# A gated sum of an FFT filter and a state-space model: the scan over odd tokens only, complex products summed on VectorE before the inverse transform, and copies of the turned x on VectorE

## The chip, the cores and the metric

The kernel runs on one core of a Trainium2 chip. The metric is device microseconds of one execution of the whole program, the median of several timed runs. Beside the timed runs there is one profiled execution; its trace gives the start and the duration of every instruction. Engines are named as the profile names them: PE is TensorE (matmuls; PEld its weight loads), DVE is VectorE, ACT is ScalarE, POOL is GpSimd, SP is SyncE, whose queue issues most of the DMAs.

## The reference

One input x of 2048 tokens by 1024 features, in bf16, goes through two branches, and a gate per token mixes them.

```python
g = sigmoid((x * gate_w).sum(-1, keepdims=True))

# branch A: a filter in the frequency domain
X = rfft2(x)                                   # 2048 x 513, complex
a = irfft2(X * (w_r + 1j * w_i), s=(2048, 1024))

# branch B: a diagonal complex state-space model, 1024 states
Lam_bar = exp(dt * Lam)
Bu = einsum("ld,pd->lp", x, ((Lam_bar - 1) / Lam)[:, None] * Bmat)
for t in range(2048):
    h = Lam_bar * h + Bu[t]
    hs.append(h)
b = 2 * einsum("lp,dp->ld", hs, Cmat).real + x * Dskip

return g * a + (1 - g) * b
```

## The kernel before

**Branch B** goes by chunks of `TC` = 256 tokens, eight of them (`c` from 0 to 7). `unit_mm` multiplies x by B on PE into PSUM, real and imaginary parts apart, and `unit_out` has ACT copy it into a tile `h` of [128, 2 (re, im), 8, 256] in bf16: 1024 states are 8 blocks of 128 partitions, and time lies along the free axis. The complex recurrence is made real by turning: a table `tab` holds, per state and per time inside the chunk, the cosine and sine of the angle that the state has turned through, so that after a rotation the recurrence has the real decay r alone. All of this is DVE's and lies in `recur`: `cross` and `along` (two products of 4096 elements per partition), `join_re` and `join_im` rotate in; `carry_in` adds the state from the chunk before into the first time step; `scan` runs h = r h + u along time, once for the real and once for the imaginary part, 2048 elements each (the decay table `rz` is zero at the first time of a block, so that one instruction goes over eight blocks); `carry_part` and `carry_sum` make the carry for the next chunk; and `cross`, `along`, `out_re`, `out_im` rotate back. Chunks 0 and 1 are done in two halves of four blocks each (`NSEP`), so these instructions are half as long there. `c_half` and `c_part` then multiply `h` by C on PE; time is the stationary side, 128 tokens (`tq`) at once.

**Branch A** is a two-dimensional FFT by matmuls. `turn` transposes x by PE into PSUM (`pt`, bf16) in 12 blocks of 128 tokens, and `turn_out` has ACT copy each into `xQ` (the last four blocks come transposed by a DMA, and ACT copies these as well). `fold` makes sums and differences on DVE, `fd` multiplies by the transform over features, `fd_out` evacuates, `s1` is the first step over tokens and `s1_out` evacuates it. By `FD_DVE` and `S1_DVE`, seven of these 32 evacuations are on DVE, the others on ACT. A turn through DRAM follows, then for eight groups `g`: `s2` on PE, `s2_out` on ACT into `X2`, `times_w` on DVE, `is1` on PE. `times_w` multiplies X (re, im) by W's real part and by its imaginary part, 2048 products per tile, two tiles `b` per group; the four kinds of product stay apart, and `is1` sums them as four accumulating steps with four variants of the matrix `MT`: 32 matmuls per group. `is2` and `is2_out` bring the result into `ZT`, and `spectral_mm`, `spectral_out`, `spectral` are the inverse transform over features, token block by token block (`tb`, 16 of 128 tokens).

**Closing.** For token blocks 0 to 9 the two branches meet through DRAM: `early_out` stores (1 - g) y, `scale_skip` and `add_skip` add the skip term to it, and `add_late` adds it to the spectral part by DMAs from POOL's queue. The last blocks meet in SBUF; blocks 13 to 15 are the end of the program: `skip_last` and `last_out` on DVE read the last C products from PSUM, and `last_store` stores them.

**Order.** Nothing is scheduled by the program that builds the kernel. Every step is a generator, and the string `ORDER` says letter by letter which one makes its next piece; `PIECES` says in which order the pieces of `recur` come (the letter `v`), and `SLOTS` which of four PSUM homes each PSUM tile takes. Each engine works through its own instructions in the order in which they were made, and each SP, ACT or POOL DMA stands in its engine's queue.

## Time and profile before

| what | value |
|---|---|
| median of 3 timed runs | 305.25 us (305.02 to 307.25) |
| profiled execution: first to last instruction | 303.6 us |
| PE busy | 296.4 us, 2568 matmuls |
| DVE busy | 289.3 us, 340 instructions |
| ACT busy | 188.5 us, 255 instructions |
| POOL busy | 73.3 us |
| granted TensorE clock | 1.00 but for the last 14 us (0.97) |
| DMA | 59.35 MB, mean 196 GB/s |

The profile gives no other time of its own than the span of its instructions; the median of the timed runs is 1.65 us above it. Busy time of PE counts overlapping matmuls once, and the ends of matmuls are modelled; DVE's busy time is the union of its instructions. A row of a group reads: line, engine, operation, written and read tiles, partitions x elements, count | total busy us, mean ns of one | idle time before.

### The profile page before, as it was taken

How to read it: one execution, taken by the hardware profiler on the slowest of the kernel's cores; microseconds unless marked ns; L12 is line 12 of the kernel's file. 1: busy time of each engine (PE TensorE's matmuls, PEld its weight loads, DVE VectorE, ACT ScalarE, POOL GpSimd, SP SyncE). 2: the span in 40 equal slices, each digit the busy share in tenths (PEclk: the TensorE clock that was granted, in tenths of full speed). 3: DMA queues.
4: the chain of work that ended last, by engine and by line, in shares of the span. 5: the costliest groups of instructions: out<-in, count | busy, mean ns of one | idle time of the engine just before them, and what ended most of it. 6: DMA issues, size and time to landing. Idle time of an engine off the chain costs nothing. (4 is left out here: it accounts for less than half of the span.)

```text
span 303.6 us, 6402 instructions
## 1 busy us (share of the span) xinstructions
PE 296.4 (98%) x2568; PEld 197.4 (65%) x2592; DVE 289.3 (95%) x340; ACT 188.5 (62%) x255; POOL 73.3 (24%) x99
## 2 busy tenths in 40 slices
PE   8999999999999999999999999999999999999995
PEld 5664677878864685458553866669657986645543
DVE  2999999999999999999999999999899999999995
ACT  4999999896532383667665865529668774343400
POOL 2100420745893001110210220202011253252330
PEclk9999999999999999999999999999999999999999
DMA  6999999989999599895948798687758876978976
GB/s 208 341 201 194 253 193 310 162 142 154 268 214 241 160 259 219 181 250 189 212 96 258 163 223 225 139 294 147 242 174 185 165 88 135 160 132 143 165 153 181
DMA packets 74157, 59.35 MB, mean 196 GB/s; under 512 B 44904, under 2 KB 61680, under 8 KB 74128
## 3 DMA queue, kind: packets, MB, share of 16 engines
q1 hardware_dynamic: 66560, 49.82, 65.8%
q0 software_dynamic: 6912, 8.69, 23.0%
q10 hardware_dynamic: 656, 0.44, 0.5%
q8 instruction: 20, 0.33, 0.4%
q14 instruction: 9, 0.07, 0.1%
HBM read 27.46 MB, written 23.08 MB: 166 GB/s over the span
## 5 line engine op out<-in xcount | busy, mean ns | idle before, releaser
L398 PE MATMUL psu<-xQ,BT 128*128 128x256 bf16 x1024 | 116.5, 273 | 0.2 <-DVE X L449 0.2
L398 PEld LDWEIGHTS <-BT 128*128 128x128 bf16 x1024 | 99.0, 98 | 17.3 <-issue 4.6
L713 PE MATMUL ps_y<-CT,h 128*128 128x512 bf16 x397 | 92.5, 379 | 0.9
L363 DVE TENSOR_TENSOR_SCAN h<-rz,h 128x2048 bf16<-128x2048 f32 (+1 forms) x20 | 70.8, 3561 | 0.0
L713 PEld LDWEIGHTS <-h 128*128 128x128 bf16 x416 | 39.6, 98 | 46.3 <-issue 2.9
L785 POOL DMA_DIRECT2D y_scratch<-su x20 | 17.3, 902 | 135.7 <-ACT su L779 105.4
L408 ACT CAST h<-psu 128x1024 bf16<-128x1024 f32 x32 | 32.3, 1011 | 18.7 <-PE psu L398 13.1
L350 DVE TENSOR_TENSOR h<-h,tab 128x4096 bf16<-128x4096 bf16 (+1 forms) x20 | 37.1, 1859 | 0.1
L744 ACT ACTIVATE ye<-ps_y,omg 128x512 f32<-128x512 f32 x26 | 17.9, 689 | 26.3 <-PE ps_y L713 11.8
L347 DVE TENSOR_TENSOR xQ<-h,tab 128x4096 bf16<-128x4096 bf16 x12 | 27.4, 2284 | 1.0 <-ACT h L408 1.0
L603 ACT CAST X<-ps_s 128x1024 bf16<-128x1024 f32 x16 | 16.2, 1010 | 14.6 <-PE ps_s L594 11.2
L727 PE MATMUL ps_q<-CT,h 128*128 128x512 bf16 (+2 forms) x110 | 21.3, 348 | 0.2
L817 ACT ACTIVATE BT<-ps_id,gB 128x1024 bf16<-128x1024 f32 x14 | 15.3, 1114 | 9.9 <-PE ps_id L810 5.7
L671 ACT CAST ZT<-ps_is 128x1024 bf16<-128x1024 f32 x16 | 15.8, 1017 | 6.2 <-PE ps_is L661 6.2
L637 ACT CAST C<-ps_is 128x1024 bf16<-128x1024 f32 x16 | 15.7, 1011 | 5.1 <-DMA xQ<-in_A_x_dram 3.4
L851 POOL DMA_DIRECT2D BT<-y_scratch x10 | 13.1, 1452 | 19.7 <-DVE BT L846 13.3
L727 PEld LDWEIGHTS <-h 128*128 128x128 bf16 x112 | 10.3, 98 | 10.4 <-DVE h L378 0.5
L779 ACT ACTIVATE su<-xs,omg 128x512 f32<-128x512 bf16 x20 | 14.2, 723 | 4.1 <-DMA y_scratch<-su 2.2
L929 ACT COPY xQ<-pt 128x1024 bf16<-128x1024 bf16 x12 | 12.2, 1082 | 1.3 <-PE pt L919 1.3
L449 ACT CAST X<-ps_fd 128x1024 bf16<-128x1024 f32 x12 | 12.3, 1062 | 1.0 <-PE ps_fd L439 0.9
L617 DVE TENSOR_TENSOR UV<-X,Wb 128x2048 bf16<-128x2048 bf16 x8 | 9.6, 1220 | 0.6 <-ACT ye L744 0.6
L617 DVE TENSOR_TENSOR UV<-X,raw 128x2048 bf16<-128x2048 bf16 x8 | 9.8, 1223 | 0.2 <-ACT X L604 0.2
(200 smaller groups left out, 397.3 us busy)
## 6 DMA issues: line engine op xcount, KB each, us to landing
y_scratch<-ye SPq DMA_DIRECT2D x20, 256.0 KB, 4.6
y_scratch<-su POOLq DMA_DIRECT2D x20, 256.0 KB, 4.7
Bb<-turn_scratch SPq DMA_DIRECT2D x16, 256.0 KB, 5.2
turn_scratch<-C SPq DMA_DIRECT2D x16, 256.0 KB, 4.1
raw<-turn_scratch SPq DMA_DIRECT2D x8, 512.0 KB, 4.3
xs<-in_A_x_dram SPq DMA_DIRECT2D x13, 256.0 KB, 3.9
out_dram<-BT SPq DMA_DIRECT2D x11, 256.0 KB, 4.3
CT<-in_A_x_dram SPq DMA_DIRECT2D x5, 512.0 KB, 6.1
```

The costliest lines, as they stand in the source:

```text
L347: nc.vector.tensor_mul(out=tmps["s"], in0=u[:, ::-1], in1=bc(i))
L350: nc.vector.tensor_mul(out=u, in0=u, in1=bc(i))
L363: nc.vector.tensor_tensor_scan(out=seg, data0=rz[:, js.start + j:js.start + j + m].rearrange("p j t -> p (j t)"), data1=seg, initial=0.0, ...
L398: nc.tensor.matmul(psu[:, j, :], lhsT=BT[4 * q + j][:, ri, d8, :], rhs=xQ[:, c, d8, :], start=(d8 == 0), stop=(d8 == 7))
L408: nc.scalar.copy(out=hs[c][:, ri, 4 * q:4 * q + 4].rearrange("p b (q j) -> p b q j", j=32), in_=psus.pop((c, q, ri)).rearrange("p b (j q) ...
L603: nc.scalar.copy(out=X2, in_=ps2s[g][b])
L617: nc.vector.tensor_mul(out=UV, in0=X2s.pop((g, b)).unsqueeze(1).to_broadcast([P, 2, 2, K]), in1=fft["Wb"][g // 2 % 2][:, :, at:at + 1, :]. ...
L671: nc.scalar.copy(out=ZT[:, 4 * kp:4 * kp + 4, :, 4 * G:4 * G + 4].rearrange("p (c r) n g -> p c r n g", c=2), in_=pszs.pop((G, kp)).rearra ...
L713: nc.tensor.matmul(psy, lhsT=hs[c][:, ri, jb, P * tq:P * (tq + 1)], rhs=CT[ri][:, jb, 512 * dh:512 * (dh + 1)], start=(i == 0), stop=(i == ...
L727: nc.tensor.matmul(psq, lhsT=hs[c][:, ri, jb, P * tq:P * (tq + 1)], rhs=CT[ri][:, jb, at:at + n], start=(i == 0), stop=(i == 15))
L744: nc.scalar.activation(out=ye, in_=psys[tb][:, K * hf:K * (hf + 1)], func=ACT.Copy, scale=omg[:, tb:tb + 1])
L785: nc.gpsimd.dma_start(out=y_dram[tb, hf], in_=xgs[tb, hf], accum_op=ALU.add)
```

## The change

Tokens are now split into even and odd ones throughout. `h` becomes [128, 2 (even, odd), 2 (re, im), 8, 128], `tab` and `rz` likewise, and a block of 128 tokens (`tb`) is the even or the odd half of a chunk: `rows_of` picks every second row of x and of the output, still whole rows of 2 KB. In `recur`, the rotation in is as before. The odd part's table holds the extra factor for one step of decay, so that `fold_in` adds the even part to the odd part; `scan` then runs over the odd tokens alone, with the decay r squared, real and imaginary part in one instruction of 2048 elements (chunks 0 and 1: two instructions of 512 per half). `next_` has ACT write r squared times the scanned value of the odd token before into a spare tile, block by block (eight ACT instructions per chunk, four per half), and `fill_in` adds that to the even part on DVE. `carry_in` puts the carry into the spare tile's first column and `carry_add` adds the same column to the odd part; `carry_sum` is gone. The rotation back is as before.

`make_tab` makes these tables: ACT scales the odd half by r, POOL casts the even half and scales the odd half by the inverse of r squared (`rinv2`), and DVE's four instructions per pair of blocks are as many and as long as before.

`times_w` takes both tiles of a group in one product of 4096 elements per partition, and then DVE makes the complex product's real part (a subtraction) and imaginary part (an addition), 1024 elements each. `is1` sums two steps instead of four: 16 matmuls per group in place of 32, with three variants of `MT`. The tiles `X2` and `UV` are twice as large and have one buffer each instead of two. `is2` and `is2_out` write `ZT` in another layout.

x is loaded by halves of 16 tokens (`x_v`), so that `pt` comes out of the transposes in the order in which `turn_out` reads it; all 16 copies of the turned x move from ACT to DVE (`TURN_DVE`), and all the evacuations of `fd` and `s1` that were on DVE move to ACT. `ORDER`, `PIECES` and `SLOTS` are written anew for all engines.

```diff
-FD_DVE = (2, 4, 6, 7)
-CAST_ACT = (5, 6, 7)
+FD_DVE = ()
-S1_DVE = (1, 4, 5)
+S1_DVE = ()
+TURN_DVE = tuple(range(16))
...
 PIECES = (
-    0, 1, 2, 3, 4, 5, 6, 8, 7, 9, 11, 10, 24, 25, 27, 26, 12, 13, 15, 14, 17, 16, 28, 18,
+    0, 1, 3, 2, 5, 6, 4, 8, 9, 10, 7, 11, 12, 14, 13, 15, 16, 17, 18, 20, 21, 19, 24, 23, 25, 22, 26, 27, 28, 29, 30,
...
-        MT=b16(np.concatenate([-np.cos(angM), -np.sin(angM), np.cos(angM), np.sin(angM)], axis=2)),
+        MT=b16(np.concatenate([-np.sin(angM), np.cos(angM), np.sin(angM)], axis=2)),
...
-    out2 = out[0]
+    rows_of = lambda t: [t.rearrange("(c p e) d -> c e p d", p=P, e=2)[tb // 2, tb % 2] for tb in range(16)]
+    out_rows, x_rows = rows_of(out[0]), rows_of(x)
...
-    x_v = x.rearrange("(p j) d -> p j d", j=16)
+    x_v = x.rearrange("(s g j) d -> g s j d", g=2, j=16)
...
     def make_tab(jp):
...
-        cast(2 * jp)(out=tab[:, 1, js, :], in_=sn_f)
-        yield
-        t1 = tmp.tile(sh, FP32, name="t1")
-        t2 = tmp.tile(sh, FP32, name="t2")
-        for j in range(2):
-            nc.scalar.activation(out=t1[:, j], in_=sn_f[:, j], func=ACT.Copy, scale=ci[:, 2 * jp + j:2 * jp + j + 1])
-        yield
-        cast(2 * jp + 1)(out=tab[:, 0, js, :], in_=cs_f)
-        yield
+        nc.gpsimd.tensor_copy(out=tab[:, 0:2, 0, js, :], in_=sc[:, :, :, 0:TS])
+        yield
+        t = tmp.tile([P, 2, 2, TC], FP32, name="t")
         for j in range(2):
             jb = 2 * jp + j
-            nc.scalar.activation(out=t2[:, j], in_=cs_f[:, j], func=ACT.Copy, scale=ci[:, jb:jb + 1])
-        yield
+            odd = sc[:, :, j, TS:TC]
+            nc.scalar.activation(out=odd, in_=odd, func=ACT.Copy, scale=r_sb[:, jb:jb + 1])
+            nc.scalar.activation(out=t[:, j], in_=sc[:, :, j], func=ACT.Copy, scale=ci[:, jb:jb + 1])
+            yield
         for j in range(2):
             jb = 2 * jp + j
-            nc.vector.scalar_tensor_tensor(out=tab[:, 2, jb, :], in0=cs_f[:, j], scalar=cr[:, jb:jb + 1], in1=t1[:, j],
-                                           op0=ALU.mult, op1=ALU.subtract)
-            yield
...
+            nc.gpsimd.tensor_scalar_mul(out=tab[:, 0:2, 1, jb, :], in0=sc[:, :, j, TS:TC], scalar1=rinv2[:, jb:jb + 1])
+            yield
+        one = lambda z: z.rearrange("p (e s) -> p e s", e=2)
+        for i, op in ((0, ALU.subtract), (1, ALU.add)):
+            for j in range(2):
+                jb = 2 * jp + j
+                nc.vector.scalar_tensor_tensor(out=tab[:, 2 + i, :, jb, :], in0=one(sc[:, i, j]), scalar=cr[:, jb:jb + 1],
+                                               in1=one(t[:, j, 1 - i]), op0=ALU.mult, op1=op)
+                yield
...
     def recur(c, js, home):
...
-        def carry_in():
-            on_in.tensor_add(out=u[:, :, :, 0], in0=u[:, :, :, 0], in1=carry[:, :, js])
-
-        def scan(ri, j, m):
-            seg = u[:, ri, j:j + m].rearrange("p j t -> p (j t)")
-            nc.vector.tensor_tensor_scan(out=seg, data0=rz[:, js.start + j:js.start + j + m].rearrange("p j t -> p (j t)"),
-                                         data1=seg, initial=0.0, op0=ALU.mult, op1=ALU.add)
+        def carry_in():
+            first = tmps["s"][:, 0, :, :, 0]
+            if c:
+                nc.vector.tensor_add(out=first, in0=ck[:, :, 0, js], in1=ck[:, :, 1, js])
+            else:
+                nc.vector.memset(first, 0.0)
+
+        def carry_add():
+            nc.vector.tensor_add(out=u[:, 1, :, :, 0], in0=u[:, 1, :, :, 0], in1=tmps["s"][:, 0, :, :, 0])
+
+        def fold_in():
+            nc.vector.tensor_add(out=u[:, 1], in0=u[:, 1], in1=u[:, 0])
+
+        def scan():
+            flat = lambda t, i: t[:, i, js].rearrange("p j t -> p (j t)") if n < 8 else t.rearrange("p r j t -> p (r j t)")
+            for i in range(2 if n < 8 else 1):
+                seg = flat(hs[c][:, 1], i)
+                nc.vector.tensor_tensor_scan(out=seg, data0=flat(rz, i), data1=seg, initial=0.0, op0=ALU.mult, op1=ALU.add)
+
+        def next_(j):
+            for i in range(j, j + 2):
+                nc.scalar.activation(out=tmps["s"][:, 0, :, i, 1:TS], in_=u[:, 1, :, i, 0:TS - 1], func=ACT.Copy,
+                                     scale=r2_sb[:, js.start + i:js.start + i + 1])
+
+        def fill_in():
+            nc.vector.tensor_add(out=u[:, 0], in0=u[:, 0], in1=tmps["s"][:, 0])
...
-        work.extend((lambda: scan(0, 0, n), lambda: scan(1, 0, n)))
+            work.append(carry_add)
+        work.extend((fold_in, scan))
         if c + 1 < NCH:
-            work.extend((carry_part, carry_sum))
+            work.append(carry_part)
+        work.extend(partial(next_, j) for j in range(0, n, 2))
+        work.append(fill_in)
         work.extend((lambda: cross(3), lambda: along(2), out_re, out_im))
...
     def times_w():
         for g in range(8):
-            for b in range(2):
-                UV = UVs[g, b] = fft["gt"].tile([P, 2, 2, K], BF16, name="UV", tag="guv", bufs=2)
-                at = 2 * (g % 2) + b
-                nc.vector.tensor_mul(out=UV, in0=X2s.pop((g, b)).unsqueeze(1).to_broadcast([P, 2, 2, K]),
-                                     in1=fft["Wb"][g // 2 % 2][:, :, at:at + 1, :].to_broadcast([P, 2, 2, K]))
-                yield
+            UV = UVs[g] = fft["gt"].tile([P, 2, 2, 2, K], BF16, name="UV", tag="guv", bufs=1)
+            W = fft["Wb"][g // 2 % 2][:, :, 2 * (g % 2):2 * (g % 2) + 2]
+            nc.vector.tensor_mul(out=UV, in0=X2s.pop(g).unsqueeze(1).to_broadcast([P, 2, 2, 2, K]),
+                                 in1=W.unsqueeze(2).to_broadcast([P, 2, 2, 2, K]))
+            yield
+            nc.vector.tensor_sub(out=UV[:, 0, 0], in0=UV[:, 0, 0], in1=UV[:, 1, 1])
+            yield
+            nc.vector.tensor_add(out=UV[:, 0, 1], in0=UV[:, 0, 1], in1=UV[:, 1, 0])
+            yield
 
     def is1():
...
-            for i, (u, r, n) in enumerate(((0, 0, 64), (0, 1, 32), (1, 0, 32), (1, 1, 0))):
+            for r in range(2):
...
     def turn_out():
         for j in range(16):
-            if j >= NTURN:
-                nc.scalar.copy(out=x_gjq[:, :, :, :, j, :].rearrange("p c d g q -> p d g c q"),
-                               in_=xt[:, j - NTURN].rearrange("p d g (c q) -> p d g c q", c=NCH))
-                yield
-                continue
-            nc.scalar.copy(out=x_gjq[:, :, :, :, j, :].rearrange("p c d g q -> p d c g q"),
-                           in_=pts.pop(j).rearrange("p d (c q g) -> p d c g q", c=NCH, g=2))
+            if j < NTURN:
+                src = pts.pop(j).rearrange("p d (g c q) -> p d g c q", g=2, c=NCH)
+            else:
+                src = xt[:, j - NTURN].rearrange("p d g (c q) -> p d g c q", c=NCH)
+            (nc.vector.tensor_copy if j in TURN_DVE else nc.scalar.copy)(
+                out=x_gjq[:, :, :, :, j, :].rearrange("p c d g q -> p d g c q"), in_=src)
             yield
```

How the instructions move is shown at three places. In these rows `x` after a row counts equal rows that follow each other, and a scan is named SCALAR_TENSOR_TENSOR with `rz` as its first operand.

DVE before, last chunk, from the first scan (L363) to the second; L825 to L846 are the spectral part of other token blocks (`BT` is reused as their home):

```order
L363 SCALAR_TENSOR_TENSOR h<-rz,h 128x2048
L844 TENSOR_TENSOR BT<-BT 128x2x512
L846 TENSOR_TENSOR BT<-BT 128x2x512
L825 TENSOR_TENSOR BT<-BT 128x2x2x128
L827 TENSOR_TENSOR BT<-BT 128x2x2x128
L836 TENSOR_TENSOR BT<-BT 128x4x256
L838 TENSOR_TENSOR BT<-BT 128x4x256
L363 SCALAR_TENSOR_TENSOR h<-rz,h 128x2048
```

DVE with the change, last chunk, from the only scan (L366) to `fill_in` (L374); L842 to L863 are the same spectral steps:

```order
L366 SCALAR_TENSOR_TENSOR h<-rz,h 128x2048
L853 TENSOR_TENSOR BT<-BT 128x4x256
L855 TENSOR_TENSOR BT<-BT 128x4x256
L861 TENSOR_TENSOR BT<-BT 128x2x512
L863 TENSOR_TENSOR BT<-BT 128x2x512
L842 TENSOR_TENSOR BT<-BT 128x2x2x128
L844 TENSOR_TENSOR BT<-BT 128x2x2x128
L853 TENSOR_TENSOR BT<-BT 128x4x256
L855 TENSOR_TENSOR BT<-BT 128x4x256
L374 TENSOR_TENSOR h<-h,xQ 128x2048
```

The second scan is gone; between the scan and the addition that needs ACT's copies of it stand eight spectral instructions.

ACT with the change, at the same place: the eight copies of `next_` (L370) for the last chunk, among the evacuations of C products (L761) and of the spectral matmuls (L834):

```order
L834 ACTIVATE BT<-ps_id,gB 128x1024 x3
L761 ACTIVATE ye<-ps_y,omg 128x512
L370 ACTIVATE xQ<-h,r_sb 128x2x127 x6
L761 ACTIVATE ye<-ps_y,omg 128x512
L370 ACTIVATE xQ<-h,r_sb 128x2x127 x2
L761 ACTIVATE ye<-ps_y,omg 128x512
```

These eight rows are new on ACT, and one evacuation stands between the sixth and the seventh of them.

DVE with the change, first half of chunk 1, from `fold_in` (L360) to the rotation back (L338); `Bcol` belongs to a small side computation of branch A, and L378 is `carry_part`:

```order
L360 TENSOR_TENSOR h<-h 128x2x512
L366 SCALAR_TENSOR_TENSOR h<-rz,h 128x512 x2
L560 COPY Bcol<-aps 32x128
L561 TENSOR_SCALAR Bcol<-Bcol 32x64
L378 TENSOR_TENSOR ck<-h,rot 128x4x4
L374 TENSOR_TENSOR h<-h,su 128x2x512
L338 TENSOR_TENSOR su<-h,tab 128x2048
```

Before, the same half chunk had two scans of 1024 elements and no `fold_in` or `fill_in`; here three small instructions stand between the scan and `fill_in`, which needs four copies from ACT.

More of the change, by code (lines that the diff above doesn't have):

```diff
@@ L1 @@
-import itertools
+from functools import partial
 from contextlib import ExitStack
@@ L27 @@
 NCH = S // TC
+TS = TC // 2
 NEARLY = 10
@@ L1091, in turn_vectors @@
         nc.scalar.activation(out=r_sb, in_=are, func=ACT.Exp)
+        nc.scalar.activation(out=r2_sb, in_=are, func=ACT.Exp, scale=2.0)
+        nc.scalar.activation(out=rinv2, in_=are, func=ACT.Exp, scale=-2.0)
         yield
```

150 lines of the change are left out of this document (73 added, 77 removed), and 11 rows, old and new, of the table PIECES.

## The prediction

> **What bounds the kernel now.** I read the busy times first, then the stretches, the waits and the chain that ended last. The page's first part (busy us, share of the span, instructions):
>
> ```profile
> PE 296.4 (98%) x2568; PEld 197.4 (65%) x2592; DVE 289.3 (95%) x340; ACT 188.5 (62%) x255; POOL 73.3 (24%) x99
> ```
>
> Two engines are close to full. The stretches show where (columns: length, then PE, PEld, DVE, ACT and POOL busy with their instructions, granted clock, DMA share, GB/s):
>
> ```profile
> 40.00:290.00 250.00, 248.83 (x2171) 167.40 (x2189) 245.85 (x247) 153.35 (x208) 62.82 (x67) 1.00 0.89 191
> 0.00:40.00 40.00, 37.20 (x337) 24.47 (x341) 33.21 (x80) 35.15 (x48) 8.39 (x31) 1.00 1.03 236
> ```
>
> Between 40 and 290 us PE is idle for 1.2 us and DVE for 4.2. Neither has room for the other's work to grow. In the first 40 us ACT is the fuller of the two copying engines. DVE's waits (us, times, longest) say the same: the one at the start apart, all are a microsecond or less.
>
> ```profile
> DVE vecF L1082 <- PE vps L1080: 4.9, 1, 4.9
> DVE xQ L347 <- ACT h L408: 1.0, 1, 1.0
> ...
> DVE UV L617 <- ACT ye L744: 0.6, 1, 0.6
> ```
>
> The chain that ended last, in order of time (start, us, what), is DVE's own work up to the end of the last chunk's rotation, then PE's last products with C:
>
> ```profile
> 283.53 1.22 DVE h L374
> 284.75 0.33 DVE BT L825
> 285.08 0.34 DVE BT L827
> 285.42 1.15 DVE h L378
> 286.56 0.05 issue
> 286.61 5.79 PE ps_q L727 x26
> 292.39 0.05 issue
> 292.44 7.99 PE ps_q L727 x52
> 300.43 0.02 issue
> 300.46 0.35 DVE raw L899
> ```
>
> So the end is the time at which DVE has done everything ahead of L378, 286.6 us, plus 17 us of PE, a last addition and its store, which the change does not touch. Work counts in full on DVE ahead of that point, and in full on PE; a saving on one engine alone is worth little.
>
> **DVE, part by part.** The groups, with shapes kept apart:
>
> ```profile
> L363 DVE TENSOR_TENSOR_SCAN h<-rz,h 128x2048 bf16<-128x2048 f32 x12 | 52.7, 4416 | 0.0
> L363 DVE TENSOR_TENSOR_SCAN h<-rz,h 128x1024 bf16<-128x1024 f32 x8 | 18.1, 2278 | 0.0
> L347 DVE TENSOR_TENSOR xQ<-h,tab 128x4096 bf16<-128x4096 bf16 x12 | 27.4, 2284 | 1.0 <-ACT h L408 1.0
> L353 DVE TENSOR_TENSOR h<-h,xQ 128x2048 bf16<-128x2048 bf16 x6 | 7.3, 1222 | 0.0
> L844 DVE TENSOR_TENSOR BT<-BT 128x1024 bf16<-128x1024 bf16 x7 | 4.8, 685 | 0.2
> L617 DVE TENSOR_TENSOR UV<-X,raw 128x2048 bf16<-128x2048 bf16 x8 | 9.8, 1223 | 0.2 <-ACT X L604 0.2
> L449 DVE CAST X<-ps_fd 128x1024 bf16<-128x1024 f32 x4 | 4.9, 1216 | 0.0
> L474 DVE CAST CT<-ps_s 128x1024 bf16<-128x1024 f32 x3 | 3.6, 1216 | 0.0
> L929 ACT COPY xQ<-pt 128x1024 bf16<-128x1024 bf16 x12 | 12.2, 1082 | 1.3 <-PE pt L919 1.3
> L943 DVE TENSOR_TENSOR preT<-xQ 128x1024 bf16<-128x1024 bf16 x6 | 4.5, 747 | 0.4 <-ACT xQ L929 0.2 <-PE pt L919 0.2
> ```
>
> An instruction holds DVE for a little less than its duration, because the next one starts before it ends. The order of time on DVE shows by how much:
>
> ```profile
> 111.19 1.22 DVE L350 TENSOR_TENSOR h<-h,tab 128x2048 bf16<-128x2048 bf16 x1
> 112.32 1.22 DVE L617 TENSOR_TENSOR UV<-X,Wb 128x2048 bf16<-128x2048 bf16 x1
> 113.46 0.23 DVE L359 TENSOR_TENSOR h<-h,carry 128x16 bf16<-128x16 bf16 x1
> ```
>
> The starts lie 1.14 us apart, so I take 0.08 off every duration: a scan of 2048 costs 4.34 us, of 1024 2.20, a product of 4096 2.20, of 2048 1.14, an addition of 1024 0.60. A scan of 512 is not in the trace; 1024 elements more cost 2.14 us (4.416 - 2.278), so 512 fewer than 1024 cost 1.07 less: 1.13.
>
> - Scans: 12 x 4.34 + 8 x 2.20 = 69.7 us now; six chunks with one scan of 2048 and four halves with two of 512 make 6 x 4.34 + 8 x 1.13 = 35.1. Gain 34.6.
> - `fold_in` and `fill_in`: 12 additions of 2048 and eight of 1024, 12 x 1.14 + 8 x 0.60 = 18.5 more.
> - `times_w`: 16 x 1.14 = 18.2 become 8 x 2.20 + 16 x 0.60 = 27.2, so 9.0 more.
> - The seven evacuations that go to ACT: 7 x 1.14 = 8.0 less.
> - Carries: 26 tiny instructions become 27, the clamp of the decay is one more; 0.2 more at the 0.1 that L359's row leaves until the next start.
> - The 16 copies of turned x have no row on DVE. From above they cost what DVE takes for 1024 elements out of PSUM, 1.14 (L449, L474), but those rows read f32; from below 0.60, its addition of as many bf16 elements, which reads two operands. L943 reads `xQ` in the runs of eight elements in which the copies write it, at 747 ns on average. I take 0.60 for the twelve from PSUM, whose 16-bit source lies in reading order after the new loading, and 0.45 for the four from SBUF, between the 0.33 of an addition of 512 elements (L825 in the chain) and 0.60: 12 x 0.60 + 4 x 0.45 = 9.0 more. All at 1.14 would be 18.2.
>
> The Trainium skill ("VectorE: DVE Perf Modes", The perf-mode tier table and the mode descriptions ahead of it) says that a copy out of PSUM reaches at most two elements a cycle, for 16-bit data in steps of one, and f32 out of PSUM one. No run here shows the first; the f32 rows above agree with the second (1024 elements in 1216 ns). By its 0.96 GHz the twelve copies would be an estimated 0.5 us each beside a fixed part, and the sum would stay where it is.
>
> Sum: -34.6 + 18.5 + 9.0 - 8.0 + 0.2 + 9.0 = -5.9 us of DVE work (with the copies at 1.14, +3.3). Nearly all of it lies ahead of the last rotation, so it counts.
>
> **New waits on DVE.** `fill_in` needs what ACT copies after the scan. The nearest row for such a copy, 254 elements with a per-partition scale, is L292's:
>
> ```profile
> 53.91 0.90 ACT L292 ACTIVATE t<-sn_f,ci 128x256 f32<-128x256 f32 x2
> 54.71 0.61 ACT L294 CAST tab<-cs_f 128x512 bf16<-128x512 f32 x1
> ```
>
> Two take 0.80 until the next starts, so 0.40 each: eight take 3.2 us, four 1.6. Against that stands what the order places between scan and `fill_in` on DVE. In the first half of chunk 1 it is three small instructions, whose rows are
>
> ```profile
> 85.92 0.27 DVE L547 COPY Bcol<-aps 32x128 bf16<-32x128 bf16 x1
> 86.22 0.24 DVE L548 TENSOR_SCALAR Bcol<-Bcol 32x64 bf16<-32x64 bf16 x1
> ```
>
> and a carry product, some 0.5 us together: a wait of 1.1 to 1.2. In the last chunk it is eight spectral instructions, 6 x 0.60 + 2 x 0.34 = 4.3 us, against 3.2 and one evacuation of 0.6: covered, barely. I count 2 us for all eight chunks, with 0 as the lower bound and 8 as the upper (each chunk late by one ACT evacuation of about 1 us). Everything behind `fill_in` on DVE waits with it, and PE waits for the rotated `h`. That leaves -3.9 us on DVE.
>
> **PE.** `is1` halves its matmuls:
>
> ```profile
> L629 PE MATMUL ps_is<-UV,raw 32*64 32x512 bf16 x256 | 8.6, 380 | 0.0
> ```
>
> Each lasts 380 ns but many overlap: 256 take 8.6 us together, 34 ns apiece, so 128 fewer are 4.3 us less. The other counts are unchanged. On PE's side the gain is -4.3, nearly DVE's.
>
> **ACT** gets 64 copies of 0.40 (25.6 us) and seven evacuations at about 0.95; it loses 16 copies of about 0.95 (the L929 row less its overlap). Its total goes from 188.5 to some 205 of 300 us. I cost this at nothing but for the waits above: with two thirds of its time full, a late copy is what remains. In the first 40 us, where it had 35 us of work, it gets lighter. The single buffers of `X2` and `UV` cost nothing where other DVE work of 3 us or more stands between two groups, which it does in nearly all; uncovered, each would cost a matmul group of 0.5 us. DMAs keep their sizes: rows of 2 KB go in and out as before.
>
> **Sum.** Both engines lose about 4 us; the lesser saving, DVE's 3.9, decides, and the span goes from 303.6 to 299.7. The median stands 1.65 us above the profiled span, so 301.3.
>
> **The rivals.**
>
> - *The copies of turned x are dear (slower).* Place: DVE's first 25 us. At 1.14 us each the DVE sum is +3.3, with the waits +5.3: about 310. Break-even is at 9.0 + 3.9 = 12.9 us for the sixteen, 0.93 for each of the twelve if the four stay at 0.45. For it: every DVE row out of PSUM in the trace is at the full price. Against: all of those read f32. Chance 0.10.
> - *The detour over ACT takes the gain back.* ACT is in order; before a chunk's eight copies stand evacuations that wait for PE. With the 8 us bound, DVE ends 2 us later than now, with half of it 2 us earlier: 303 to 307, 305 in the middle. For it: the 0.5 us cover of chunk 1 and the 4.3 of the last chunk. Against: in chunks 2 to 6 there are 7 to 14 us of DVE work between. Chance 0.22.
> - *POOL makes the tables late.* Before the first rotation POOL must now make three table pieces of the second pair of blocks instead of two. POOL's rows
>
> ```profile
> 86.18 0.24 POOL L539 TENSOR_TENSOR AB<-Wh 128x32 f32<-128x32 f32 x1
> 86.39 6.90 POOL L540 TENSOR_TENSOR AB<-Wh 128x32 f32<-128x32 f32 x1
> ```
>
>   show the same instruction at 0.24 and, while DVE ran additions and products, at 6.90 us. One such hold on a table piece would delay the first rotation by some 4 us of uncovered time: no gain, about 305. Chance 0.06. The Trainium skill ("SBUF — State Buffer", Who interferes with whom) states this as a rule: VectorE with two SBUF inputs and a reading GpSimd exclude each other on a shared port. The two rows agree with it.
> - *More than the sum.* If ACT's relief lets PE fill the 2.8 us that it idles in the first 40 us, PE's side is -7.1 and DVE, with no wait, -5.9 and an earlier first instruction (its 4.9 us wait at the start shrinks, as the first transposed block is ready before `vps`): about 298.5. Chance 0.14.
> - *The forecast:* 299 to 302.5. Chance 0.48.
>
> **The numbers.** The likeliest is 301.3. Below 298 I leave some 6%, above 307 some 13%: range 298 to 307. One per cent, about what a measurement of this kernel tells from no change, is 302.2 and 308.3. Faster: nine tenths of the forecast (0.43), all of the last rival (0.14), a little of the detour (0.03): 0.60. Slower: most of the dear copies (0.08) and the worst of the detour and of POOL (0.02): 0.10. The rest, 0.30, is no change.
>
> **What would show it.** Right: the copies of `xQ<-pt` on DVE near 0.7 us; the scans' group near 36 us; `ps_is` of `is1` near 4.3; DVE's busy time near 283 with waits for ACT's `su` and `xQ` of 2 us in all; the last rotation (L378 before) done near 282.7 us; PE and DVE both still over 94%. Wrong: copies over 0.93 us; waits for L370 above 6 us; a first rotation that waits for POOL; or PE losing its 4.3 us to waits for `UV`, whose way from product to matmul is now three instructions long.

## The result and the profile after

The changed kernel takes 363.23 us (median of 4 runs, 362.33 to 363.6) beside 305.77 us for the kernel before on the same chip: 1.188 times as long, 95% interval 1.184 to 1.192. The prediction said 301.3 us. Its profiled execution spans 361.6 us against 303.6.

Three places of the two traces split the 58.0 us. DVE's first rotation in (L347 before, L338 now) starts at 99.1 us instead of 42.2, so 56.9 us are lost ahead of it. From there to the end of the last rotation back (L378, now L385) it is 242.5 us instead of 244.4, 1.9 us less. Behind it stand 20.0 us instead of 17.0, 3.0 us more.

The page of the kernel after: the busy times, then 40 slices of the span (busy share in tenths, PE's granted clock in tenths, the share of the DMA engines).

```profile
PE 305.8 (85%) x2464; PEld 200.7 (56%) x2464; DVE 288.8 (80%) x373; ACT 207.1 (57%) x309; POOL 70.6 (20%) x106
...
PE   3420565096999999999999999999989999999896
...
DVE  0412724028999998999999999999999899999993
...
PEclk9975769578999999999999999999999999999999
DMA  1141119599999999899768869957799972789986
```

Before, two engines were close to full from end to end. Now PE is busy for less than 70% of each of the first eight slices (72 us) and DVE for less than half of seven of them, the DMAs' share is below two tenths in five of the first six, and from the eleventh on the page looks as it did before. The stretches say how empty (columns: length, then PE, PEld, DVE, ACT and POOL busy, granted clock, DMA share, GB/s):

```profile
0.00:20.00 20.00, 8.54 (x54) 5.30 (x54) 4.86 (x18) 3.11 (x9) 2.55 (x15) 1.00 0.13 47
20.00:40.00 20.00, 5.68 (x40) 4.44 (x41) 4.74 (x13) 0.83 (x2) 0.00 (x0) 0.57 0.27 87
```

A share of 0.13 is that of two DMA engines out of sixteen at work all the time. It moves 47 GB/s, where the first 40 us before went at 236 (the row of the prediction). PE waits for x, and DVE for PE's transposes of it; the last row is the wait for ACT's copies that the prediction counted (us in total, times, longest):

```profile
DVE xQ L945 <- PE pt L936: 52.2, 9, 12.9
...
PE pt L936 <- DMA CT<-in_A_x_dram: 31.8, 6, 8.2
...
DVE h L374 <- ACT su L370: 1.9, 2, 1.3
```

SP's queue in order of time (start, duration, line) shows that the loads hold up whatever stands behind them: L245 are the loads of x, L255 the transform G, L241 x's transposes by DMA, L250 the second matrix of branch A.

```profile
1.96 9.06 SPq L245 DMA_DIRECT2D CT<-in_A_x_dram  x3
11.06 12.63 SPq L255 DMA_DIRECT2D G_sb<-c_G  x3
23.74 21.37 SPq L245 DMA_DIRECT2D CT<-in_A_x_dram  x3
45.15 23.47 SPq L241 DMA_TRANSPOSE CT<-in_A_x_dram  x1
68.67 0.57 SPq L250 DMA_DIRECT2D raw<-c_T  x1
```

Three issues of G take 12.6 us and one transpose 23.5 us on the queue, while the seven loads of x in the kernel before took 0.33 to 0.72 us each to issue (the view of their line, L242). Of what the prediction costed piece by piece, the scans (36.3 us in all) and the copies are there nearly to the figure; `is1` takes 5.1 us where it named 4.3. The groups of the kernel after (busy us, mean ns | idle before):

```profile
L366 DVE TENSOR_TENSOR_SCAN h<-rz,h 128x2048 bf16<-128x2048 f32 x6 | 26.5, 4419 | 0.1
...
L366 DVE TENSOR_TENSOR_SCAN h<-rz,h 128x512 bf16<-128x512 f32 x8 | 9.8, 1261 | 0.1
...
L945 DVE COPY xQ<-pt 128x1024 bf16<-128x1024 bf16 x12 | 8.2, 689 | 52.2 <-PE pt L936 52.2
...
L646 PE MATMUL ps_is<-UV,raw 32*64 32x512 bf16 x128 | 5.1, 386 | 0.0
```

### The profile page after: what moved, and what is told of

Read it like the earlier page. It is cut to its first block, busy times and chain, and to the rows that moved or that the text cites. A ratio compares the mean times of both kernels' runs of the same rounds, so it can differ in the third digit from the quotient of the medians.

```text
span 361.6 us, 6239 instructions
## 1 busy us (share of the span) xinstructions
PE 305.8 (85%) x2464; PEld 200.7 (56%) x2464; DVE 288.8 (80%) x373; ACT 207.1 (57%) x309; POOL 70.6 (20%) x106
## 4 chain that ended last, share of the span: by engine, by line
PE 40%; DVE 26%; SPq 17%; DMA 9%; issue 4%; ACT 3%; POOL 0%; DVEq 0%; ACTq 0%
PE psu L408 17%; PE ps_y L730 15%; SPq L241 6%; SPq L245 6%; DMA CT<-in_A_x_dram 6%; DVE h L341 5%; PE ps_q L744 4%; SPq L255 3%; DVE su L338 2%; DMA raw<-ye 2%; DVE h L366 2%; DVE h L374 1%; DVE xQ L338 1%; DVE h L385 1%; PE ps_is L679 1%
## 5 line engine op out<-in xcount | busy, mean ns | idle before, releaser
L408 PEld LDWEIGHTS <-BT 128*128 128x128 bf16 x1024 | 99.1, 98 | 16.5 <-issue 4.4
L730 PEld LDWEIGHTS <-h 128*128 128x128 bf16 x416 | 39.8, 98 | 47.8 <-issue 3.5
L945 DVE COPY xQ<-pt 128x1024 bf16<-128x1024 bf16 x12 | 8.2, 689 | 52.2 <-PE pt L936 52.2
L802 POOL DMA_DIRECT2D y_scratch<-su x20 | 18.5, 1034 | 129.2 <-ACT su L796 110.0
L936 PE MATMUL pt<-ident,CT 128*128 128x128 bf16 x96 | 11.0, 296 | 31.8 <-DMA CT<-in_A_x_dram 31.8
L341 DVE TENSOR_TENSOR h<-h,tab 128x4096 bf16<-128x4096 bf16 (+1 forms) x20 | 37.3, 1869 | 0.3
L366 DVE TENSOR_TENSOR_SCAN h<-rz,h 128x512 bf16<-128x512 f32 (+1 forms) x14 | 36.3, 2614 | 0.2
L761 ACT ACTIVATE ye<-ps_y,omg 128x512 f32<-128x512 f32 x26 | 17.3, 683 | 25.6 <-DMA raw<-ye 10.4
L936 PEld LDWEIGHTS <-CT 128*128 128x128 bf16 x96 | 8.8, 136 | 37.0 <-DMA CT<-in_A_x_dram 34.5
L459 ACT CAST X<-ps_fd 128x1024 bf16<-128x1024 f32 x16 | 15.8, 1023 | 21.7 <-PE ps_fd L453 21.6
L338 DVE TENSOR_TENSOR xQ<-h,tab 128x4096 bf16<-128x4096 bf16 x12 | 27.4, 2280 | 0.3 <-ACT h L418 0.3
L487 ACT CAST CT<-ps_s 128x1024 bf16<-128x1024 f32 x8 | 8.0, 1011 | 27.4 <-PE ps_s L472 27.4
L370 ACT ACTIVATE xQ<-h,r_sb 128x254 bf16<-128x254 bf16 x48 | 20.9, 503 | 3.7 <-DVE h L366 3.6
L472 PE MATMUL ps_s<-X,raw 64*128 64x512 bf16 x64 | 11.2, 470 | 12.2 <-DMA raw<-c_T 12.2
L868 POOL DMA_DIRECT2D BT<-y_scratch x10 | 12.2, 1465 | 32.3 <-ACT BT L834 16.1
```

Source lines behind the costliest of these rows:

```text
L338: nc.vector.tensor_mul(out=tmps["s"], in0=u[:, :, ::-1], in1=bc(i))
L341: nc.vector.tensor_mul(out=u, in0=u, in1=bc(i))
L366: nc.vector.tensor_tensor_scan(out=seg, data0=flat(rz, i), data1=seg, initial=0.0, op0=ALU.mult, op1=ALU.add)
L370: nc.scalar.activation(out=tmps["s"][:, 0, :, i, 1:TS], in_=u[:, 1, :, i, 0:TS - 1], func=ACT.Copy, scale=r2_sb[:, js.start + i:js.start + ...
L408: nc.tensor.matmul(psu[:, j, :], lhsT=BT[4 * q + j][:, ri, d8, :], rhs=xQ[:, c, d8, :], start=(d8 == 0), stop=(d8 == 7))
L730: nc.tensor.matmul(psy, lhsT=hs[c][:, tq, ri, jb, :], rhs=CT[ri][:, jb, 512 * dh:512 * (dh + 1)], start=(i == 0), stop=(i == 15 and tb not ...
```

## The experiments

The first theory (A): the loads by halves, `x.rearrange("(s g j) d -> g s j d", g=2)`, give each DMA an outermost dimension of 2, and so only two DMA engines carry it. The seven loads move 2 x 256 + 5 x 512 KB, 3.15 MB: 67 us at 47 GB/s against 12 us at the 264 GB/s of before's first 20 us, and the difference of 55 us is nearly the delay. The rivals: the new order on SP's queue (B), rows that are read 32 apart (B too), or the new compute (C).

**One number of the load changed.**

```diff
-    x_v = x.rearrange("(s g j) d -> g s j d", g=2, j=16)
+    x_v = x.rearrange("(s g j) d -> g s j d", g=16, j=16)   # or g=4
```

> The changed kernel with one number different: the loads of x take their rows as 16 groups of 8 (outermost dimension 16) instead of 2 groups of 64; bytes, row length, count of loads, order on every queue stay. Tokens of the loaded blocks thereby land in other columns, so what is computed is not the reference. Theory A (an outermost dimension of 2 lets only 2 of the 16 DMA engines carry a load; the trace of the changed kernel shows a DMA share of 0.13 = 2/16 and 47 GB/s in the first 20 us): the loads are carried by all 16, the DMA share of the first 20 us rises to 0.8 or more, the first rotation (L338) starts near 42 us instead of 99, and the time is 300 to 307. Theory B (the new order on the SP queue, or the reading of rows 32 apart instead of 16, is what is slow): the time stays at 355 to 363. Theory C (the changed compute itself is slower by much of the 57 us): 330 or more with the first rotation at 42 us.

> As the run with an outermost dimension of 16, but with 4 groups of 32 rows (the output is again not the reference's, since tokens land in other columns). Theory A: a share of 0.25 of the DMA engines, some 94 GB/s in the first 20 us; the 3.1 MB of x that are loaded this way take about 33 us instead of 67, so about 33 us of the 57 come back: 325 to 338. Theory B: 355 to 363. A result between 300 and 310 would say that there is a threshold, not a share.

Measured: 310.45 us with 16 groups, 334.79 us with 4; the first rotation starts at 44.8 and 68.4 us. The first 20 us of the two kernels, 16 groups first:

```profile
0.00:20.00 20.00, 16.25 (x142) 9.83 (x143) 14.61 (x45) 9.08 (x17) 2.54 (x15) 1.00 0.92 214
```

```profile
0.00:20.00 20.00, 9.19 (x70) 5.88 (x70) 6.88 (x23) 3.94 (x10) 2.54 (x15) 0.79 0.39 113
```

47, 113 and 214 GB/s for 2, 4 and 16, with bytes, issues and order unchanged and the same rows in other places: theory A stands, B and C fall for the bulk. 310.45 us is 3 us above the upper end that A gave, so something smaller is lost besides.

The Trainium skill ("DMA: Bandwidth & Descriptors", Why a DMA increments its semaphore by 16 and not by 1) says that a DMA runs on the largest number of engines up to 16 that divides the slowest dimension of both of its access patterns, and its Rules for kernel authors warn of an outermost dimension under 16. The three shares here, 0.13, 0.39 (with other DMAs in it) and 0.92, agree with it.

The DMA packets in the traces agree too. In the changed kernel from 26 to 34 us, when the loads of x have the DMAs nearly to themselves (share 0.13, 51 GB/s), two packets are under way for 96% of the time. From 3 to 9 us four at once is the commonest count with 4 groups, and sixteen with 16 groups. In the kernel before it is sixteen as well (3 to 12 us).

**The load alone, in the kernel before.**

```diff
-    x_v = x.rearrange("(p j) d -> p j d", j=16)
+    x_v = x.rearrange("(s g j) d -> g s j d", g=2, j=16)
```

> The kernel before with one part of the change alone: x loaded by halves in one DMA for each two blocks (outermost dimension 2), and ACT's copy out of PSUM read in the order that follows from it; all else, the order of every queue too, as before. Theory A: the load alone costs the whole loss, DMA share 0.13 in the first 20 us, 350 to 365. Theory B (queue order): 304 to 308, no change.

Measured: 356.83 us, 1.169 times before (1.166 to 1.172), first rotation at 93.2 us. This load alone (with ACT's copy out of PSUM read in the order that follows from it) costs the kernel before 51.8 us of the 57.5. The new order of SP's queue isn't needed for it. The DMA share of its first 20 us is 0.24, not 0.13 as expected; in this order G and other transfers stand between the loads of x.

**The load mended, in two ways.** First two DMAs per load:

```diff
-                nc.sync.dma_start(out=xn[i][:, js], in_=x_v[:, :, 2 * i + js.start:2 * i + js.stop, :])
+                for g in range(2):
+                    nc.sync.dma_start(out=xn[i][64 * g:64 * (g + 1), js], in_=x_v[g, :, 2 * i + js.start:2 * i + js.stop, :])
```

> The changed kernel with each load of x split into two DMAs, one for each half, whose outermost dimension is 64 rows (the rows read and their places stay as in the changed kernel, so the output is the reference's). Theory A: all 16 DMA engines carry each load, at the price of 7 more issues on SP (some 0.4 us each, 3 us in the start): first rotation at 42 to 46 us, time 300 to 309; in it VectorE's copies of turned x, the scans and the products cost what they cost in the changed kernel, so it also shows whether the predicted 3.9 us are there. Theory B (reading rows 32 apart, or queue order): 355 to 363.

Then before's load, with the halves made by the transposes:

```diff
-    x_v = x.rearrange("(s g j) d -> g s j d", g=2, j=16)
+    x_v = x.rearrange("(p j) d -> p j d", j=16)
...
-                nc.sync.dma_start(out=xn[i][:, js], in_=x_v[:, :, 2 * i + js.start:2 * i + js.stop, :])
+                nc.sync.dma_start(out=xn[i][:, js], in_=x_v[:, 2 * i + js.start:2 * i + js.stop, :])
...
+    ident_gs = ident.rearrange("p (s g) -> p g s", g=2)
...
-                nc.tensor.transpose(out=pt[:, i, :], in_=xn[j // 2][:, j % 2, P * i:P * (i + 1)], identity=ident)
+                nc.tensor.transpose(out=pt[:, i, :], in_=xn[j // 2][:, j % 2, P * i:P * (i + 1)], identity=ident_gs)
```

> The changed kernel with x loaded as in the kernel before (one DMA per two blocks, the 128 partitions outermost, so no more issues on SP than before), and the order by halves made in the transposes instead: their identity matrix is read with its columns in the order even, odd. The output is the reference's. Two runs with spread loads stood at 310.5 and 311.6 us, some 5 us above the kernel before; their traces put this down to 2.7 us up to the first rotation (L338 at 44.6 us against 41.9), a gain of 1.4 us between first and last rotation, and 3.1 us behind the last rotation. Theory D (the rest of the change costs these 5 us whatever the load): 308.5 to 311, first rotation near 44.5. Theory E (the rows' new order in memory or the extra issues still cost something at the start): 305 to 307.5, first rotation at 42.

Measured: 311.58 us with two loads, above what was expected, though rows 32 apart are read here as well, so the distance of the rows isn't what was slow; 307.89 us with the permuted identity, 1.010 times before (1.007 to 1.014), between the ranges of the two theories. So the load cost 363.2 - 307.9 = 55.3 us. Its first rotation starts at 42.7 us, so the extra 2 to 3 us at the start of the two earlier runs were their loads' (theory E in that part). The rest is at the end: 20.0 us behind the last rotation, as in the changed kernel. The end of its chain (start, us, what):

```profile
277.15 0.61 DVE BT L863
278.04 0.44 POOL BT L868
279.01 0.47 issue
279.48 8.39 DMA raw<-ye
287.96 0.70 ACT ye L761
288.70 14.03 PE ps_q L744 x80
```

POOL's queue holds an addition of y (L901) behind two others (L868) that wait for DVE; its landing releases one of two `ye` buffers, which ACT's last evacuation needs, which PE needs.

**That place in POOL's queue.**

```diff
-    "...ooOpovzzZQQBOYYZ9ZZD9..."
+    "...ooOpovzzZBQQOYYZ9ZZD9..."
```

> As the run with the permuted identity, with one letter of the order moved: the fourth of own_add's DMAs (L901, raw<-ye) stands ahead of the two add_late DMAs on POOL's queue instead of behind them. In the trace with spread loads it waits there until 279.9 us for DVE's L863, lands at 290.0, and only then ACT's last ye and with it PE (idle for 2.0 us at 290.5) go on. Theory F (the 3.1 us behind the last rotation come from this place in POOL's queue): the DMA goes out some 4 us earlier, PE's idle 2.0 us there go, and the time falls by 1.5 to 2.5 us against the run with the permuted identity. Rival (the landing of 8.5 us is what is late, whenever it is issued, or DVE is the bound there anyway): less than 0.7 us.

Measured: 305.22 us, 1.001 times before (0.999 to 1.004), 2.7 us less than without. In the trace the end behind the last rotation falls from 20.0 to 18.1 us; before's 17.0 is not reached, and the 1.1 us between stay open. The DMA goes out 3.75 us before the two that it stood behind, and PE's wait for ACT at that place is gone (POOL of this kernel):

```profile
275.98 0.86 POOL L901 DMA_DIRECT2D raw<-ye  x1 [2.18 <-ACT ye L761]
279.73 2.44 POOL L868 DMA_DIRECT2D BT<-y_scratch  x2 [2.89 <-DVE BT L863]
```

So the changed kernel's loss is two edits, one line of the load and one letter of the order. With both mended it is as fast as before, and still not 3.9 us faster. The other runs ask why.

**Who copies the turned x.** With the permuted identity, all copies on ACT; then, with POOL's DMA moved too, the split of before.

```diff
-TURN_DVE = tuple(range(16))
+TURN_DVE = ()
```

```diff
-FD_DVE = ()
+FD_DVE = (2, 4, 6, 7)
-S1_DVE = ()
+S1_DVE = (1, 4, 5)
-TURN_DVE = tuple(range(16))
+TURN_DVE = ()
```

> As the run with the permuted identity, but all 16 copies of turned x are ACT's again, in the same places of the order. DVE loses 9.0 us of work, all of it ahead of the first rotation; ACT, busy for 28 of the first 40 us, gets some 15 us more. Theory G (DVE's work is what sets the start, as the prediction counted it): the first rotation comes 4 to 9 us earlier, and the time falls to 301 to 306. Rival (ACT becomes the bound of the first 40 us, since the seven evacuations are ACT's too): first rotation at 44 to 50 us, 309 to 315.

> As the run with POOL's DMA moved (305.2 us), with the split of the copies as in the kernel before: the 16 copies of turned x on ACT, and seven evacuations of fd and s1 on DVE. By durations DVE's work ahead of the first rotation stays nearly the same (9.0 us go, 8.0 come), ACT gets some 9 us more than in the run with POOL's DMA moved and 7 us less than in the run with all copies on ACT (326.1). Theory J (the split is a wash once ACT has room, as the prediction's sum for DVE says): 305 to 309, first rotation at 42 to 46 us. Theory K (ACT's time, or DVE's waits for ACT's copies, set the start in this order): 312 to 322, first rotation at 49 to 56 us.

Measured: 326.06 us (first rotation at 59.3 us), above the ranges of both theory G and its rival, and 316.58 us (53.2 us), as theory K had it. In this order ACT sets the start as soon as it has these copies. With all of them on ACT, its group and DVE's wait for it read:

```profile
L947 ACT COPY xQ<-pt 128x1024 bf16<-128x1024 bf16 x12 | 11.9, 1043 | 1.9 <-PE pt L938 1.9
```

```profile
DVE preT L961 <- ACT xQ L947: 15.7, 4, 5.0
```

1043 ns on ACT against 681 ns on DVE with the same reading order. Moving them is worth 18.2 us in this order and cost DVE 8.6. The order before got the same first rotation out of the old split, so these figures hold for the new order only.

**The detour over ACT.** `next_` left out:

```diff
-                nc.scalar.activation(out=tmps["s"][:, 0, :, i, 1:TS], in_=u[:, 1, :, i, 0:TS - 1], func=ACT.Copy,
-                                     scale=r2_sb[:, js.start + i:js.start + i + 1])
```

> As the run with the permuted identity, but ACT's copies of the scanned odd tokens (next_, L370, 64 instructions, 27.8 us of ACT) are left out, so the even tokens are wrong; fill_in stays on DVE. It prices the detour over ACT. Prediction's step (2 us of waits on DVE): the time falls by 1 to 3 us against the run with the permuted identity. Rival (the detour costs more, through ACT's evacuations that come late behind these copies): it falls by 4 us or more.

Measured: 306.87 us, 1.0 us less than with it; the intervals of the two against before overlap (1.004 to 1.008 and 1.007 to 1.014). The detour is cheap, far from the rival's 4 us.

**A wait on DVE, and the complex sum.** One letter later for L786; `times_w` without its subtraction and addition, with before's four sums in `is1`; both.

```diff
-    "...JJY%vIIviyhvvviNJhINv+..."
+    "...JJY%vIIvihvvvyiNJhINv+..."
```

```diff
-            nc.vector.tensor_sub(out=UV[:, 0, 0], in0=UV[:, 0, 0], in1=UV[:, 1, 1])
-            nc.vector.tensor_add(out=UV[:, 0, 1], in0=UV[:, 0, 1], in1=UV[:, 1, 0])
...
-            for r in range(2):
+            for i, (u, r, n) in enumerate(((0, 0, 64), (0, 1, 32), (1, 0, 32), (1, 1, 0))):
```

> As the run with POOL's DMA moved (305.2 us), with one more letter moved: the product of a skip tile with D (L786), for which DVE waits 2.75 us at 231.4 (its xs comes late behind SP's queue), stands three instructions later on DVE, behind L341, L385 and L381. Theory H (DVE sets the pace there): the time falls by 1.5 to 2.8 us, to 302.4 to 303.7. Rival (PE sets it, or the wait comes back at the next instruction that needs ACT): it falls by less than 0.7 us.

> As the run with POOL's DMA moved (305.2 us), with the complex sum undone: the sixteen instructions L633 and L635 on DVE (9.6 us) go, and is1 sums four products on PE as before (256 matmuls instead of 128, 8.6 us against 5.1). Everything else stays. Theory I (DVE alone is the bound of the changed kernel; PE has room): the time falls by 5 to 9 us, to 296 to 300. The prediction's view (both engines are full, the lesser saving decides, so PE's 3.5 us come back): 305 to 309.

> Both edits together: four products on PE, and the skip product later on DVE. If DVE is the bound throughout, the two gains add (another 1.5 to 2.8 us below the run with four products); if PE has become the bound by the first, the second is worth less than 0.7 us.

Measured: 305.48 us (1.001 of before, 0.999 to 1.003), 309.37 us (1.010, 1.007 to 1.014) and 308.22 us (1.009, 1.005 to 1.012). The wait on DVE was worth nothing. Giving DVE back 9.6 us of work and PE its 3.4 us made the program some 3 to 4 us longer (2.7 by the ratios to before, 4.2 by the medians), so DVE alone isn't the bound. The group on PE with four products:

```profile
L644 PE MATMUL ps_is<-UV,raw 32*64 32x512 bf16 x256 | 8.6, 380 | 0.0
```

The third run doesn't tell more: 1.1 us between the two is no more than their spread.

**One engine lighter, the other, and both.** All three on the kernel with POOL's DMA moved:

```diff
         def fill_in():
-            nc.vector.tensor_add(out=u[:, 0], in0=u[:, 0], in1=tmps["s"][:, 0])
+            pass
```

```diff
     def c_half(psy, tb, dh):
...
-        for i in range(16):
+        for i in range(14):
```

> As the run with POOL's DMA moved (305.2 us), but fill_in (L374, ten additions on DVE, 9.7 us of its work, with its 2.6 us of waits for ACT) is left out, so the even tokens are wrong; nothing of PE changes. Theory P (PE sets the pace between the first and the last rotation): the time falls by less than 3 us, and PE's idle stays near 5 us. Theory V (DVE sets it): it falls by 7 to 12 us.

> As the run with POOL's DMA moved (305.2 us), but c_half sums 14 of 16 products (52 matmuls of 0.216 us each, 11.2 us of PE, are left out, so branch B lacks an eighth of its states for blocks 0 to 12); nothing of DVE changes, and the last products behind the last rotation stay. Theory P: the time falls by 5 to 11 us, until DVE is full. Theory V: it falls by less than 3 us, as PE only waits more.

> Both at once: fill_in is left out (9.7 us of DVE, the even tokens are wrong) and c_half sums 14 of 16 products (11.2 us of PE, an eighth of the states is missing there). Each alone stood at 304.5 and 306.0 us beside 305.2, so neither engine alone sets the pace. Theory Q (both engines are full, and only a saving on both shortens the program): 295 to 299 us. Rival (a third thing, such as the DMAs or the tail's queue, sets the pace): 302 us or more.

Measured: 304.45 us without `fill_in` (0.996 of before, 0.993 to 0.998), 305.95 us with 14 products (1.000, 0.997 to 1.003), 301.78 us with both (0.989, 0.987 to 0.992). Neither P nor V holds by itself: 9.7 us off DVE gave 0.8, 11.2 us off PE gave nothing, both gave 3.4. The stretch from 45 to 280 us, which lies between the first and the last rotation but for at most 2 us, shows where the savings went (columns as above; in this order with L786 moved, without `fill_in`, with 14 products, with both):

```profile
45.00:280.00 235.00, 232.22 (x1971) 157.48 (x1969) 228.55 (x248) 167.57 (x255) 52.47 (x63) 1.00 0.84 193
45.00:280.00 235.00, 231.32 (x1957) 157.84 (x1972) 221.07 (x239) 168.29 (x257) 52.67 (x63) 1.00 0.87 194
45.00:280.00 235.00, 223.89 (x1920) 154.40 (x1936) 230.09 (x250) 169.38 (x258) 51.72 (x63) 1.00 0.87 193
45.00:280.00 235.00, 228.18 (x1952) 155.83 (x1951) 226.50 (x245) 171.86 (x261) 54.49 (x65) 1.00 0.90 197
```

Of the 235 us PE is idle for 2.8 us with L786 moved, 3.7 without `fill_in`, 11.1 with 14 products and 6.8 with both; DVE for 6.5, 13.9, 4.9 and 8.5. The engine that alone is made lighter mostly waits for the other.

From the first rotation to the last the traces have 243.2 us with the permuted identity and 243.1 with L786 moved, 241.3 without `fill_in`, 241.2 with 14 products, and 235.7 with both: 1.9 and 2.0 us less for one engine, 7.5 for both. (The kernel with POOL's DMA moved, on which the three are built, has 244.8; but its profiled execution, 307.41 us, was the longest of its ten, so those two stand in for it.) So in this stretch both engines are nearly full: a saving of some 10 us on one shortens it by 2, on both by 7.5.

Of these 7.5 us 3.4 are left in the timed median: behind the last rotation it takes about 1 us more (19.1 instead of 18.1), and the profiled execution was the shortest of its kernel, 2.5 us under the median. Some of PE's saving may have gone into the granted clock: the two executions at a mean clock of 1.0 took 303.8 and 304.2 us with 14 products, and 299.3 and 300.9 with both, so about 1 and 5 us less than the kernel that they are built on. These are two executions each. The median of 301.78 lies between the two expectations, close to the rival's 302, and with both lighter PE and DVE still idle for 6.8 and 8.5 us, so a third thing may have a share; the stretch in the traces speaks for theory Q.

## Why the prediction was wrong

**The step that failed** is the last sentence on ACT: "DMAs keep their sizes: rows of 2 KB go in and out as before." Sizes and rows did stay. What changed was the shape of the access pattern, whose outermost dimension went from 128 partitions to 2, and with it the load went from sixteen packets under way at a time to two, and from a DMA share of 0.96 in the first 20 us to 0.13. The term was nothing in the sum and measured 55.3 us (51.8 by itself in the kernel before). There was no rival for it: the load was read as preparation for `turn_out`, not as an edit with a price, although the diff shows it.

**The second step that failed:** 17 us behind the last rotation, "which the change does not touch". The order there was written anew too, and one DMA on POOL's queue came to stand behind two that wait: 3.0 us more. Moving it gave 1.9 of them back in the trace and 2.7 us in the timed median.

**The rest of the sum: 3.9 us forecast, nothing found.** The profile of the kernel with both mended and L786 moved spans 303.7 us, as long as before's 303.6, so the two can be laid side by side. DVE's time by start to start, idle taken out, forecast and measured:

| step on DVE | forecast, us | measured, us |
|---|---|---|
| scans | -34.6 | -34.2 |
| `fold_in` and `fill_in` | +18.5 | +19.5 |
| `times_w` | +9.0 | +9.3 |
| evacuations to ACT | -8.0 | -8.0 |
| copies of turned x | +9.0 | +8.6 |
| carries | +0.2 | +1.5 |
| `cross` and `along` | 0 | +1.6 |
| all others | 0 | 0.0 |
| work | -5.9 | -1.7 |
| idle | +2.0 | +1.8 |

The big terms held to within a microsecond; 4.2 us are lost in all, most of it in small terms, and DVE's busy time, forecast near 283 us, is 287.7. One reason is the 0.08 us that the prediction took off every duration. It came from instructions that don't touch each other's data. DVE of the mended kernel in order of time shows both sorts:

```profile
75.97 0.69 DVE L381 TENSOR_TENSOR h<-h,su 128x1024 bf16<-128x1024 bf16 x1
76.58 0.70 DVE L385 TENSOR_TENSOR h<-h,su 128x1024 bf16<-128x1024 bf16 x1
77.31 1.23 DVE L338 TENSOR_TENSOR su<-h,tab 128x2048 bf16<-128x2048 bf16 x1
78.57 1.23 DVE L341 TENSOR_TENSOR h<-h,tab 128x2048 bf16<-128x2048 bf16 x1
79.83 0.74 DVE L344 TENSOR_TENSOR h<-h,su 128x1024 bf16<-128x1024 bf16 x1
```

L385 starts 0.08 us before L381's end. L341 overwrites what L338 reads and starts 0.03 us behind its end, as L344 does behind L341. That the shared data are the reason is read from such rows, not tested by a run. The new order puts such pairs side by side more often (the next instruction overlapped 36 of the 40 `cross` and `along` before, and 22 here): `cross` and `along` cost 1.6 us more, and `fold_in` and `fill_in` 1.0 more. The carries cost 1.3 us more than forecast, 0.7 of it behind two memsets ahead of `fill_in`'s wait, in time that isn't counted as idle. The forecast of 2 us for waits on ACT's copies held: 1.9 us in the changed kernel, 3.0 in the mended one, and 1.0 us of time.

**PE** got its saving: by start to start `is1` takes 4.6 us instead of 8.0, 3.4 less where 4.3 were forecast (31 ns apiece before by this count, 36 now, instead of 34 for both), and undoing it cost some 3 to 4. Against that stand 1.1 us more in other groups (0.6 in the transposes) and 2.4 us more idle. In both figures 0.9 us are put right that the trace of the kernel before shows as idle: 17 matmuls of `c_half` have no record there, and each leaves a gap of 0.05 us. That both engines are nearly full and a saving on one is worth little, as the prediction had it, is what the last three runs speak for. DVE's saving of 1.7 us was nothing once its 1.8 us of idle are counted, and PE's of 2.3 (3.4 less 1.1) nothing beside its 2.4.

**The rivals.** The dear copies of turned x didn't come: 689 ns out of PSUM in the changed kernel, near the 0.68 that 0.60 and the overlap make, and far from 1.22 for f32. The Trainium skill's rule ("VectorE: DVE Perf Modes", The perf-mode tier table) that a copy out of PSUM reaches at most two elements a cycle for 16-bit data and one for f32 agrees with that pair of rows. The detour over ACT cost about 1.0 us. No wait of DVE for POOL's tables is among the rows of the mended kernel. The gain of PE's idle time in the first 40 us didn't come either: there it idles for 2.8 us before and 2.1 in the mended kernel with L786 moved. The prediction's "in the first 40 us, where it had 35 us of work, it gets lighter" was costed at nothing; in the new order it is what the order is built on (18.2 us without it).

## What to carry to other kernels

Read a changed `rearrange` in a DMA as a change of that DMA: look at the outermost dimension of both sides, not at bytes and row length, and price a small one at the rate of a few engines (47 GB/s for two here). If an order of rows is wanted that would make that dimension small, make it elsewhere; a permuted identity in a transpose that runs anyway cost next to nothing here. Where two engines are full, sum the small terms on both, and treat the places behind the last bound (the tail's queues) as part of the change when the order is rewritten.

## What the runs showed of the hardware that was not expected

- **Throughput followed the outermost dimension of the load.** 47, 113 and 214 GB/s in the first 20 us for 2, 4 and 16, with the same bytes. The Trainium skill's rule, quoted with those runs, names the cause, and the counts of packets under way agree with it; the traces don't say which engines carried them.
- **A slow load holds the queue behind it, not only its readers.** Issues that took 0.3 to 0.7 us before took up to 10.7 us (L245), and a transpose behind them 23.5 us (11.4 in the run with 16 groups).
- **Reading the identity with a column step of two cost PE nothing that shows.** A transpose took 219 to 234 ns on average in the runs with the permuted identity, and 221 to 229 with the plain one where the load was fast. The group in the first run with the permuted identity, and in the kernel before:

```profile
L938 PE MATMUL pt<-ident,CT 128*128 128x128 bf16 x96 | 7.0, 219 | 1.3 <-DMA CT<-in_A_x_dram 1.3
```

```profile
L919 PE MATMUL pt<-ident,CT 128*128 128x128 bf16 x96 | 7.6, 229 | 0.3 <-ACT xQ L929 0.3
```

- **A lower granted clock went with a PE that waits.** All executions of the kernel before had a mean granted clock of 0.998 to 1.0. The changed kernel had 0.925 to 0.972, the one with 14 products 0.983 to 1.0. With both engines lighter, the executions at 1.0 took 299.3 and 300.9 us and those at 0.989 to 0.994 took 301.8 to 302.4. That the lower clock is caused by PE's waits is read from this company, not shown by a run of its own.
